# A head that takes the cosine and sine tiles in turn for two rows of x

## The chip, the cores and the metric

The kernel runs on one core of one Trainium2 chip. The core has a matrix engine (TensorE, in the profile PE, with PEld for its weight loads), a vector engine (VectorE, DVE), a scalar engine (ScalarE, ACT), a general engine (GpSimd, POOL) and a sync engine (SP) that only issues transfers. Transfers between the chip's memory and the core's working memory run on 16 DMA engines. The engines run side by side, each takes its own instructions in the order of the program, and they wait for each other through semaphores.

The metric is the device time of one execution in microseconds (us), the median of several.

## The reference

```python
def _A_ref(x, dft_seq_re, dft_seq_im, dft_hid_re, dft_hid_im):
    a = jnp.einsum("bsd,ed->bse", x, dft_hid_re)
    b = jnp.einsum("bsd,ed->bse", x, dft_hid_im)
    return jnp.einsum("ts,bse->bte", dft_seq_re, a) - jnp.einsum("ts,bse->bte", dft_seq_im, b)

def _B_ref(x, w_in, w_sp, b_sp, w_out):
    z = _gelu(jnp.einsum("bsd,df->bsf", x, w_in))
    z1, z2 = z[..., :Fh], _layernorm(z[..., Fh:], axis=-1)
    g = jnp.einsum("ts,bsf->btf", w_sp, z2) + b_sp[None, :, None]
    return jnp.einsum("bsf,fd->bsd", z1 * g, w_out)

mod = (_silu(c) @ w_mod).reshape(c.shape[0], 6, 1, -1)
sa, ca, ga, sb, cb, gb = ...
h = _layernorm(x, axis=-1) * (1 + ca) + sa
x = x + ga * _A_ref(h, ...)
h = _layernorm(x, axis=-1) * (1 + cb) + sb
x = x + gb * _B_ref(h, ...)
```

x has 2048 positions of 512 features. The first half mixes with two Fourier matrices, the second half is a gated two-layer network. Everything is float32.

## The kernel before

The first stage multiplies the normed x from the left with the cosine and the sine matrix over positions (2048 x 2048 each). x is handled in 16 "rows" s of 128 positions (X[s], 128 x 512). The matrices come in blocks of 512 x 512 (list src, in turn cosine and sine for a group of four rows; block b lies in stage[b], two buffers). A block holds four tiles k of 128 positions; tile n is the unit of the stage: `squares` transposes it from the block on DVE into T[n] (tag t, two buffers), ACT copies it to a rounded high part AH[n] (four buffers), DVE subtracts to get the low part AL[n] (three buffers). The row of x is split in the same way into h_hi[s] and h_lo[s]. Tile n then takes twelve matmuls: for each of four feature blocks high times high, high times low, low times high, added in four PSUM banks per matrix (GP). With t = 0, tiles 0 to 3 are the cosine with rows 0 to 3, tiles 4 to 7 the sine with rows 0 to 3, tiles 8 to 11 the cosine with rows 4 to 7, and so on.

Tile 0 alone isn't split (WHOLE = 1): its four matmuls take T[0] and the normed row in plain float32, which the profile shows as eight passes.

The order on each engine is written by hand (a manual schedule). Ahead of the loop stands the head, lines 1087 to 1122. It issues transfers on SP (some on ACT's queue, through `two`): row 0 of x, half of the first cosine block, row 1, rows 2 and 3, the other half, the first sine block (load(1)), rows 4 and 5. `keep_busy` puts matmuls of ones on PE until the data is there. `stats_first` takes mean and variance of a row on DVE, the power −1/2 on POOL, and the shift on DVE (row 0) or POOL. `whole_first(0)` norms row 0 on ACT; `hi_first`, `norm_x`, `lo_h` make the two parts of rows 1 to 3; `split_first(0)` and `rest_first(0)` make those of row 0, at the end of the head.

Then the loop runs over n: `prep(n)` prepares tile n + 3's high and tile n + 2's low part unless the head has done so, `mm_a(n)` issues the matmuls, and `run(n)` the work that `at(n, ...)` has put there: at 0 the load of rows 6 and 7 (load_x(1, range(2, 4))), at 2 the row c, at 4 the stats of rows 4 and 5 and the load of rows 8 to 11, at 6 the stats of rows 6 and 7 and the high parts of rows 4 and 5, at 7 the low parts of rows 4 and 5. The last tile of a block, in prep_hi, frees its buffer and issues load(b + 2). So load(2) is issued in the head (prep_hi(3)) and load(3) in the loop (prep_hi(7), at n = 4).

```python
        if not N2 <= n < N4 and k == 3:
            stage.pop(b)
            if b != NB0:
                load(b + 2)
```

Of the kernel before, what the change touches and what calls it, by code (L numbers as in the profile page):

```python
# [13 lines left out]
P = 128  # L14
# [6 lines left out]
def fnet_gmlp_kernel(  # L21
# [125 lines left out]
    NE = N4 + 4 * NQ * len(PROD)  # L147
    NB = {p: N4 + 4 * NQ * i for i, p in enumerate(PROD)}
    NB0 = len(src) + 2
    stage, T, AH, AL = {}, {}, {}, {}  # L150

    def load_block(tile_, a, s0=0, s1=P):
        v = a.rearrange("(b j) (a s) -> a j b s", j=32, a=4)
        for q in range(4):
            nc.sync.dma_start(tile_[32 * q:32 * q + 32, :, s0:s1], v[q][:, :, s0:s1])

    def load_half(tile_, a, h, engs=(nc.sync,) * 4):

        v = a.rearrange("(b j) (a s) -> a j b s", j=32, a=4)
        for q in range(4):  # L160
            engs[q].dma_start(tile_[32 * q:32 * q + 32], v[q][:, :, 64 * h:64 * h + 64])
# [3 lines left out]
    def load(b):  # L165
        if b < len(src):
            stage[b] = blocks.tile([P, 16, P], F32, tag="stage", bufs=2, name=f"stage{b}")
            load_block(stage[b], src[b])
        elif b < len(src) + 2:
            j = b - len(src)  # L170
            XB.append(blocks.tile([P, 4, Q], F32, tag="stage", bufs=2, name=f"xb{j}"))
            for g in range(2):
                nc.sync.dma_start(XB[j][:, 2 * g:2 * g + 2], ht_d[g].rearrange("(k p) t -> p k t", p=P)[:, 2 * j:2 * j + 2])
                for kk in range(2):
                    TT[2 * j + kk, g] = XB[j][:, 2 * g + kk]
        elif 4 * (b - NB0) < NE - N4:
            i, gh = divmod(b - NB0, NQ)
            g, h = divmod(gh, 2)
            p = PROD[i]
            stage[b] = blocks.tile([P, 2, 16, 64], F32, tag="stage", bufs=2, name=f"stage{b}")  # L180
            for r in range(2):
                load_half(stage[b][:, r], s_d[S_OF[p], r, g] if p in S_OF else
                          quad(w_sp, r + (2 if p == 4 else 0), g + (2 if p == 1 else 0)), h)
# [5 lines left out]
    def squares(dst, block, k):  # L189
        nc.vector.transpose(dst.rearrange("p (b i) -> p b i", i=32), block[:, :, 32 * k:32 * k + 32])  # L190
# [61 lines left out]
    def prep_hi(n):  # L252
        if n >= NE or n in highs:
            return
        highs.add(n)
        if N2 <= n < N4:
            T[n] = form_t(n)
        else:
            b, k = divmod(n, 4) if n < N2 else (NB0 + (n - N4) // 4, (n - N4) % 4)
            if b != NB0:  # L260
                T[n] = blocks.tile([P, Q], F32, tag="t", bufs=2, name=f"t{n}")
            if b == NB0:
                assert n in T
            elif n >= N4:
                squares(T[n], stage[b][:, k % 2], k // 2)
            else:
                squares(T[n], stage[b], k)
        AH[n] = SE[2][:, n - N4] if N4 <= n < N4 + 4 else blocks.tile([P, Q], F32R, tag="ah", bufs=4, name=f"ah{n}")
        nc.scalar.activation(AH[n], T[n], AF.Copy)  # L269
        if not N2 <= n < N4 and k == 3:  # L270
            stage.pop(b)
            if b != NB0:
                load(b + 2)
# [91 lines left out]
    def keep_busy(n, k):  # L365

        ps = bank(k, "busyp")
        for _ in range(n):
            nc.tensor.matmul(ps, ones, busy, start=True, stop=True)

    def fold_sum(t, w, u):

# [49 lines left out]
    def load_x(g, ks=range(4), eng=nc.sync):  # L422

        if g not in XG:
            XG[g] = spool.tile([P, 4, D], F32, tag="x", bufs=2, name=f"x{g}")
        k0, k1 = ks[0], ks[-1] + 1
        v = x.rearrange("(g a k i) d -> g a i k d", g=NQ, a=4, i=32)
        for a in range(4):
            eng.dma_start(XG[g][32 * a:32 * a + 32, k0:k1, :], v[g, a][:, k0:k1, :])
        for k in ks:  # L430
            X[4 * g + k] = XG[g][:, k, :]
# [4 lines left out]
    def stats_first(s):  # L436

        m = spool.tile([P, 12], F32, tag="first", bufs=4, name=f"first{s}")
        nc.vector.bn_stats(m[:, :6], X[s])
        mv = m[:, 8:]  # L440
        nc.vector.bn_aggr(mv[:, :2], m[:, :6])
        nc.vector.tensor_scalar(mv[:, 1:2], mv[:, 1:2], EPS, None, op0=ALU.add)
        nc.gpsimd.tensor_tensor(mv[:, 2:3], mv[:, 1:2], mhalf, op=ALU.pow)
        eng = nc.gpsimd if s else nc.vector
        eng.tensor_scalar(mv[:, 3:4], mv[:, 0:1], mv[:, 2:3], -1.0, op0=ALU.mult, op1=ALU.mult)
        NRM[s] = mv[:, 2:3], mv[:, 3:4]

    two = (nc.sync, nc.sync, nc.scalar, nc.scalar)
# [1 line left out]
    def load_two(k):  # L450
        if not k:
            XG[0] = spool.tile([P, 4, D], F32, tag="x", bufs=2, name="x0")
        v = x.rearrange("(g a k i) d -> g a i k d", g=NQ, a=4, i=32)
        for a in range(4):
            two[a].dma_start(XG[0][32 * a:32 * a + 32, k, :], v[0, a][:, k, :])
        X[k] = XG[0][:, k, :]

    def whole_first(s):

        LN[s] = spool.tile([P, D], F32, tag="xn", bufs=4, name=f"xn{s}")  # L460
        nc.scalar.activation(LN[s].rearrange("p (k a i) -> p k a i", a=4, i=32),
                             X[s].rearrange("p (a k i) -> p k a i", a=4, i=32), AF.Identity,
                             bias=NRM[s][1], scale=NRM[s][0])
        nc.scalar.activation(LN[s][:, :1], ones[:, :1], AF.Copy)

    def split_first(s):
# [3 lines left out]
    def rest_first(s):  # L470
        hh, hl = [h.rearrange("p k m -> p (k m)") for h in (h_hi[s], h_lo[s])]
        nc.gpsimd.tensor_tensor(hl, LN[s], hh.bitcast(F32), op=ALU.subtract)

    def turn_whole(n):
        T[n] = blocks.tile([P, Q], F32, tag="t", bufs=2, name=f"t{n}")
        squares(T[n], stage[0], n)
        highs.add(n)
        lows.add(n)
# [23 lines left out]
    def ones_x(s):  # L502
        LN[s] = spool.tile([P, D], F32, tag="xn", bufs=4, name=f"xn{s}")
        nc.gpsimd.memset(LN[s][:, 0:1], 1.0)
# [27 lines left out]

    def mm_a(n):
        t, r = divmod(n, 8 * NQ)
        j, s = ((r // 4) % 2, r // 8 * 4 + r % 4) if t == 0 else (r // NS, r % NS)
        if s == 0:
            for k in range(ND):
                GP[t, j, k] = bank(4 * j + k if t == 0 else ring[0] % 6, f"gp{t}_{j}_{k}")
                ring[0] += t > 0
        if n < WHOLE:  # L540
            a, b = LN.pop(s), T.pop(n)
            for k in (1, 2, 3, 0):
                nc.tensor.matmul(GP[0, 0, k], a[:, k * P:(k + 1) * P], b, start=s == 0, stop=False)
            return
        ah, al = AH.pop(n), AL.pop(n)
        if n < 4:
            for a, b in ((h_hi[s], ah), (h_hi[s], al), (h_lo[s], ah)):
                for k in (1, 2, 3, 0):
                    nc.tensor.matmul(GP[0, 0, k], a[:, k, :], b, start=False, stop=False)
            return  # L550
        for k in range(ND):
            matmul3(GP[t, j, k], h_hi[s][:, k, :], h_lo[s][:, k, :], ah, al, s == 0, s == NS - 1)
        if s == NS - 1:
            for k in range(ND):
                ps = GP.pop((t, j, k))
                gt_hi[t, j, k] = GP_[0].tile([P, Q], F32R, tag=f"gh{j}_{k}", name=f"gh{t}_{j}_{k}")
                gt_lo[t, j, k] = GP_[0].tile([P, Q], F32R, tag=f"gl{j}_{k}", name=f"gl{t}_{j}_{k}")
                split(gt_hi[t, j, k], gt_lo[t, j, k], ps)
# [526 lines left out]


    load_two(0)
    stage[0] = blocks.tile([P, 16, P], F32, tag="stage", bufs=2, name="stage0")
    load_half(stage[0][:, :, :64], src[0], 0, two)
    load_two(1)  # L1090
    nc.scalar.activation(sc, ones[:, :ND], AF.Silu)
    load_x(0, range(2, 4))
    load_half(stage[0][:, :, 64:], src[0], 1)
    load(1)
    load_x(1, range(2))
    keep_busy(3, 5)
    ones_x(1)
    ones_x(2)
    ones_x(3)
    stats_first(0)  # L1100
    whole_first(0)
    turn_whole(0)
    prep_hi(1)
    stats_first(1)
    prep_lo(1)
    hi_first(1)
    stats_first(2)
    norm_x(1)
    stats_first(3)
    hi_first(2)  # L1110
    lo_h(1)
    prep_hi(2)
    norm_x(2)
    prep_hi(3)
    prep_lo(2)
    lo_h(2)
    hi_first(3)
    norm_x(3)
    prep_lo(3)
    split_first(0)  # L1120
    rest_first(0)
    lo_h(3)
    at(0, load_x, 1, range(2, 4))
    at(2, load_row)
    at(9, silu_row)
# [324 lines left out]
```

## Time and profile before

| | us |
|---|---|
| median of three runs | 931.37 |
| the runs | 932.79, 931.37, 931.15 |
| the profiled execution | 931.77 |
| its span, first to last instruction | 930.0 |
| PE busy | 924.2 |
| DVE busy | 738.2 |
| ACT busy | 409.1 |
| POOL busy | 199.1 |

The span is what the trace covers, the time of an execution what the device reports for it. Start times in the trace count from the span's start. "Busy" of PE is the union of its matmuls, whose ends are modelled. In a row of a timeline stand the start, the duration (of the group, if several instructions are merged), the engine, the line, the operation with the tiles it writes and reads, the count, and in brackets how long the engine stood idle before it and what ended that. SPq and ACTq rows are issues of transfers.

### The profile page before, as it was taken

What the parts mean: (1) busy time and instruction counts of PE and PEld (TensorE: products, weight loads), DVE (VectorE), ACT (ScalarE), POOL (GpSimd) and SP (SyncE); (2) the same over time, 40 slices, a digit from 0 to 9 for tenths busy, and PEclk for the clock granted to TensorE, in tenths of its full rate; (3) what the DMA queues carried; (4) which work ended last, traced back from release to release, by engine and by line L of the source; (5) the groups of instructions that cost most, each with busy time, mean ns of one, the idle gap of its engine ahead of it and who ended that gap; (6) DMA issues with size and microseconds to landing.
All of it is one profiled execution on the core that took longest, in us unless ns stands there. A gap on an engine that the chain in (4) does not pass through costs nothing.

```text
span 930.0 us, 12339 instructions
## 1 busy us (share of the span) xinstructions
PE 924.2 (99%) x4053; PEld 760.4 (82%) x4053; DVE 738.2 (79%) x1218; ACT 409.1 (44%) x733; POOL 199.1 (21%) x375
## 2 busy tenths in 40 slices
PE   9999999999999999999999999999999999999998
PEld 5888888888888888888888888888888888888887
DVE  7799968787687677875678788899799789986762
ACT  5694424232132222322577877674544544331121
POOL 2330000224554165323512321331000000000000
PEclk9999999999999999999999999999999999999999
DMA  9995762856639977996463864444464566734651
GB/s 218 225 227 118 142 158 46 193 147 171 158 91 319 283 220 217 275 343 227 141 217 130 279 201 103 118 105 105 105 146 102 130 142 143 178 97 149 185 178 57
DMA packets 246976, 157.88 MB, mean 170 GB/s; under 512 B 140384, under 2 KB 214368, under 8 KB 246784
## 3 DMA queue, kind: packets, MB, share of 16 engines
q1 hardware_dynamic: 233248, 119.57, 52.2%
q0 software_dynamic: 12272, 36.86, 11.4%
q8 instruction: 32, 0.52, 0.2%
q10 hardware_dynamic: 1392, 0.66, 0.2%
q14 instruction: 32, 0.26, 0.1%
HBM read 120.33 MB, written 36.71 MB: 169 GB/s over the span
## 4 chain that ended last, share of the span: by engine, by line
PE 98%; DMA 1%; SPq 0%; ACTq 0%; DVE 0%; ACT 0%; issue 0%; DVEq 0%
PE gp L99 12%; PE gp L97 12%; PE gp L98 12%; PE gw L99 10%; PE gw L97 10%; PE gw L98 10%; PE yp L99 3%; PE yp L98 3%; PE yp L97 3%; PE op L98 3%; PE op L97 3%; PE op L99 3%; PE fp L98 1%; PE fp L97 1%; PE fp L99 1%; PE z2s L98 1%
## 5 line engine op out<-in xcount | busy, mean ns | idle before, releaser
L269 ACT ACTIVATE ah<-t 128x512 fp32r<-128x512 f32 x235 | 148.5, 632 | 362.6 <-DVE t L190 242.7
L287 DVE TENSOR_TENSOR al<-t,ah 128x512 fp32r<-128x512 f32 x235 | 160.6, 683 | 55.7 <-PE gp L98 30.9
L98 PE MATMUL gp<-al,hh 128*128 128x512 f32 x496 | 193.0, 389 | 0.0
L97 PE MATMUL gp<-ah,hh 128*128 128x512 f32 x496 | 193.0, 389 | 0.0
L99 PE MATMUL gp<-ah,hl 128*128 128x512 f32 x496 | 193.0, 389 | 0.0
L190 DVE STREAM_TRANSPOSE t<-stage 128x512 f32<-128x512 f32 x236 | 165.5, 702 | 6.3 <-DMA stage<-in_A_dft_seq_re_dram 3.1
L98 PE MATMUL gw<-al,bh 128*128 128x512 f32 x400 | 155.6, 389 | 0.0
L99 PE MATMUL gw<-ah,bl 128*128 128x512 f32 x384 | 149.5, 389 | 0.0
L97 PE MATMUL gw<-ah,bh 128*128 128x512 f32 x384 | 149.4, 389 | 0.0
L98 PEld LDWEIGHTS gp<-al,hh 128*128 128x128 f32 x496 | 93.1, 188 | 19.5 <-DVE al L287 0.2
L97 PEld LDWEIGHTS gp<-ah,hh 128*128 128x128 f32 x496 | 93.1, 188 | 19.4
L99 PEld LDWEIGHTS gp<-ah,hl 128*128 128x128 f32 x496 | 93.1, 188 | 19.3
L98 PEld LDWEIGHTS gw<-al,bh 128*128 128x128 f32 x400 | 75.1, 188 | 15.7
L99 PEld LDWEIGHTS gw<-ah,bl 128*128 128x128 f32 x384 | 72.1, 188 | 15.3 <-DVE bl L948 0.3
L97 PEld LDWEIGHTS gw<-ah,bh 128*128 128x128 f32 x384 | 72.1, 188 | 14.9
L920 POOL DMA_DIRECT2D s_d<-sj x64 | 35.1, 548 | 107.2 <-DVE sj L912 82.3
L97 PE MATMUL yp<-hth,gh 128*128 128x512 f32 x128 | 49.8, 389 | 0.0
L98 PE MATMUL yp<-htl,gh 128*128 128x512 f32 x128 | 49.8, 389 | 0.0
L99 PE MATMUL yp<-hth,gl 128*128 128x512 f32 x128 | 49.8, 389 | 0.0
L665 POOL DMA_DIRECT2D ht_d<-hturn x62 | 41.0, 667 | 23.1 <-DVE hturn L661 18.2
L97 PE MATMUL op<-woh,uh 128*128 128x512 f32 x110 | 42.8, 389 | 0.0
L98 PE MATMUL op<-wol,uh 128*128 128x512 f32 x110 | 42.8, 389 | 0.0
(247 smaller groups left out, 1449.4 us busy)
## 6 DMA issues: line engine op xcount, KB each, us to landing
stage<-in_A_dft_seq_im_dram SPq DMA_DIRECT2D x64, 256.0 KB, 6.0
sj<-in_B_w_sp_dram SPq DMA_DIRECT2D x32, 512.0 KB, 7.2
s_d<-sj POOLq DMA_DIRECT2D x64, 256.0 KB, 4.7
stage<-s_d SPq DMA_DIRECT2D x128, 128.0 KB, 2.9
stage<-in_A_dft_seq_re_dram SPq DMA_DIRECT2D x60, 256.0 KB, 5.6
stage<-in_B_w_sp_dram SPq DMA_DIRECT2D x88, 128.0 KB, 3.0
wm<-in_w_mod_dram SPq DMA_DIRECT2D x16, 256.0 KB, 6.1
xr<-in_A_x_dram POOLq DMA_DIRECT2D x16, 256.0 KB, 4.5
```

The lines of the kernel that those rows point to most:

```text
L97: nc.tensor.matmul(acc, ah, bh, start=first, stop=False, skip_group_check=go_on)
L98: nc.tensor.matmul(acc, ah, bl, start=False, stop=False, skip_group_check=go_on)
L99: nc.tensor.matmul(acc, al, bh, start=False, stop=last, skip_group_check=go_on)
L190: nc.vector.transpose(dst.rearrange("p (b i) -> p b i", i=32), block[:, :, 32 * k:32 * k + 32])
L269: nc.scalar.activation(AH[n], T[n], AF.Copy)
L287: nc.vector.tensor_tensor(AL[n], t, AH[n].bitcast(F32), op=ALU.subtract)
L665: eng.dma_start(v[a, i], ht[32 * a:32 * a + 32].rearrange("c (b r) -> c b r", r=32))
L920: nc.gpsimd.dma_start(s_d[m, r, g][b * P:(b + 1) * P, :], a)
```

## The change

The first eight tiles get an order of their own, FRONT, as pairs (matrix j, row s): cosine 0, sine 0, cosine 1, sine 1, cosine 2, cosine 3, sine 2, sine 3. The transfers follow it: row 0 of x, a quarter of the cosine block, half of the sine block, row 1, the second quarter, rows 2 and 3, the two remaining halves, rows 4 and 5. The normed row 0 is written in three pieces, the factor of the shift moves to POOL for row 0 too, one busy matmul becomes a half, the parts of row 0 are made at once, and `turn_front(n)` turns tiles 1 to 7 at places of their own. What follows a block's last turn stays with it: turn_front(5) issues load(2), turn_front(7) issues load(3), both in the head.

```diff
+    FRONT = ((0, 0), (1, 0), (0, 1), (1, 1), (0, 2), (0, 3), (1, 2), (1, 3))
...
-            b, k = divmod(n, 4) if n < N2 else (NB0 + (n - N4) // 4, (n - N4) % 4)
+            b, k = FRONT[n] if n < len(FRONT) else divmod(n, 4) if n < N2 else (NB0 + (n - N4) // 4, (n - N4) % 4)
...
-        if not N2 <= n < N4 and k == 3:
+        if not N2 <= n < N4 and k == 3 and b in stage:
...
         for _ in range(n):
             nc.tensor.matmul(ps, ones, busy, start=True, stop=True)
+        nc.tensor.matmul(ps[:, :D // 2], ones, busy[:, :D // 2], start=True, stop=True)
...
-        eng = nc.gpsimd if s else nc.vector
-        eng.tensor_scalar(mv[:, 3:4], mv[:, 0:1], mv[:, 2:3], -1.0, op0=ALU.mult, op1=ALU.mult)
+        nc.gpsimd.tensor_scalar(mv[:, 3:4], mv[:, 0:1], mv[:, 2:3], -1.0, op0=ALU.mult, op1=ALU.mult)
...
-        nc.scalar.activation(LN[s].rearrange("p (k a i) -> p k a i", a=4, i=32),
-                             X[s].rearrange("p (a k i) -> p k a i", a=4, i=32), AF.Identity,
-                             bias=NRM[s][1], scale=NRM[s][0])
+        for ks in (slice(1, 2), slice(2, 4), slice(0, 1)):
+            nc.scalar.activation(LN[s].rearrange("p (k a i) -> p k a i", a=4, i=32)[:, ks],
+                                 X[s].rearrange("p (a k i) -> p k a i", a=4, i=32)[:, ks], AF.Identity,
+                                 bias=NRM[s][1], scale=NRM[s][0])
...
+    def turn_front(n):
+        b, k = FRONT[n]
+        T[n] = blocks.tile([P, Q], F32, tag="t", bufs=2, name=f"t{n}")
+        squares(T[n], stage[b], k)
+        if k == 3:
+            stage.pop(b)
+            load(b + 2)
...
-        j, s = ((r // 4) % 2, r // 8 * 4 + r % 4) if t == 0 else (r // NS, r % NS)
+        j, s = FRONT[n] if n < len(FRONT) else ((r // 4) % 2, r // 8 * 4 + r % 4) if t == 0 else (r // NS, r % NS)
...
-        if n < 4:
-            for a, b in ((h_hi[s], ah), (h_hi[s], al), (h_lo[s], ah)):
+        if n < len(FRONT):
+            for i, (a, b) in enumerate(((h_hi[s], ah), (h_hi[s], al), (h_lo[s], ah))):
                 for k in (1, 2, 3, 0):
-                    nc.tensor.matmul(GP[0, 0, k], a[:, k, :], b, start=False, stop=False)
+                    nc.tensor.matmul(GP[0, j, k], a[:, k, :], b, start=s == 0 and i == 0, stop=False)
...
     load_two(0)
-    stage[0] = blocks.tile([P, 16, P], F32, tag="stage", bufs=2, name="stage0")
-    load_half(stage[0][:, :, :64], src[0], 0, two)
-    load_two(1)
+    for b in range(2):
+        stage[b] = blocks.tile([P, 16, P], F32, tag="stage", bufs=2, name=f"stage{b}")
+    load_block(stage[0], src[0], 0, 32, two)
+    load_block(stage[1], src[1], 0, 64, two)
     nc.scalar.activation(sc, ones[:, :ND], AF.Silu)
+    load_x(0, range(1, 2))
+    load_block(stage[0], src[0], 32, 64)
     load_x(0, range(2, 4))
-    load_half(stage[0][:, :, 64:], src[0], 1)
-    load(1)
+    load_block(stage[0], src[0], 64, P)
+    load_block(stage[1], src[1], 64, P)
     load_x(1, range(2))
-    keep_busy(3, 5)
-    ones_x(1)
-    ones_x(2)
-    ones_x(3)
+    keep_busy(2, 5)
+    for s in range(1, 4):
+        ones_x(s)
     stats_first(0)
     whole_first(0)
     turn_whole(0)
+    split_first(0)
+    rest_first(0)
+    turn_front(1)
     prep_hi(1)
     stats_first(1)
     prep_lo(1)
     hi_first(1)
+    turn_front(2)
+    turn_front(3)
+    prep_hi(2)
+    norm_x(1)
+    prep_lo(2)
+    prep_hi(3)
+    lo_h(1)
+    prep_lo(3)
     stats_first(2)
-    norm_x(1)
+    turn_front(4)
+    turn_front(5)
+    prep_hi(4)
+    hi_first(2)
+    prep_lo(4)
+    norm_x(2)
     stats_first(3)
-    hi_first(2)
-    lo_h(1)
-    prep_hi(2)
-    norm_x(2)
-    prep_hi(3)
-    prep_lo(2)
     lo_h(2)
+    prep_hi(5)
+    prep_lo(5)
     hi_first(3)
+    turn_front(6)
+    turn_front(7)
     norm_x(3)
-    prep_lo(3)
-    split_first(0)
-    rest_first(0)
+    prep_hi(6)
     lo_h(3)
+    prep_lo(6)
     at(0, load_x, 1, range(2, 4))
```

More of the change, by code (lines that the diff above doesn't have):

```diff
@@ L149, in fnet_gmlp_kernel, with load_block @@
     NB0 = len(src) + 2
+    FRONT = ((0, 0), (1, 0), (0, 1), (1, 1), (0, 2), (0, 3), (1, 2), (1, 3))
     stage, T, AH, AL = {}, {}, {}, {}
-    def load_block(tile_, a, s0=0, s1=P):
+    def load_block(tile_, a, s0=0, s1=P, engs=(nc.sync,) * 4):
         v = a.rearrange("(b j) (a s) -> a j b s", j=32, a=4)
         for q in range(4):
-            nc.sync.dma_start(tile_[32 * q:32 * q + 32, :, s0:s1], v[q][:, :, s0:s1])
+            engs[q].dma_start(tile_[32 * q:32 * q + 32, :, s0:s1], v[q][:, :, s0:s1])
     def load_half(tile_, a, h, engs=(nc.sync,) * 4):
@@ L258, in prep_hi @@
         else:
-            b, k = divmod(n, 4) if n < N2 else (NB0 + (n - N4) // 4, (n - N4) % 4)
-            if b != NB0:
+            b, k = FRONT[n] if n < len(FRONT) else divmod(n, 4) if n < N2 else (NB0 + (n - N4) // 4, (n - N4) % 4)
+            if n not in T:
                 T[n] = blocks.tile([P, Q], F32, tag="t", bufs=2, name=f"t{n}")
[L262 to L267, printed above, removed]
+                if n >= N4:
+                    squares(T[n], stage[b][:, k % 2], k // 2)
+                else:
+                    squares(T[n], stage[b], k)
         AH[n] = SE[2][:, n - N4] if N4 <= n < N4 + 4 else blocks.tile([P, Q], F32R, tag="ah", bufs=4, name=f"ah{n}")
         nc.scalar.activation(AH[n], T[n], AF.Copy)
-        if not N2 <= n < N4 and k == 3:
+        if not N2 <= n < N4 and k == 3 and b in stage:
             stage.pop(b)
@@ L472, in rest_first @@
         nc.gpsimd.tensor_tensor(hl, LN[s], hh.bitcast(F32), op=ALU.subtract)
+    def turn_front(n):
+        b, k = FRONT[n]
+        T[n] = blocks.tile([P, Q], F32, tag="t", bufs=2, name=f"t{n}")
+        squares(T[n], stage[b], k)
+        if k == 3:
+            stage.pop(b)
+            load(b + 2)
     def turn_whole(n):
```

## The prediction

> **What bounds the kernel now.** I read the page first: busy times, then the chain that ended last.
>
> ```profile
> span 930.0 us, 12339 instructions
> PE 924.2 (99%) x4053; PEld 760.4 (82%) x4053; DVE 738.2 (79%) x1218; ACT 409.1 (44%) x733; POOL 199.1 (21%) x375
> PE 98%; DMA 1%; SPq 0%; ACTq 0%; DVE 0%; ACT 0%; issue 0%; DVEq 0%
> ```
>
> TensorE (PE) is the bound, and the change alters none of the matmuls behind the first eight tiles. So I asked where PE ever waits: the view of PE's waits, then busy time by stretch.
>
> ```profile
> PE busyp L369 <- DVE busy L308: 1.5, 1, 1.5
> PE gp L549 <- ACT ah L269: 0.7, 1, 0.7
> ...
> 13.54:14.25 0.71, 0.00 (x1) 0.00 (x0) 0.61 (x3) 0.68 (x2) 0.00 (x0) 1.00 1.27 232
> 14.26:450.00 435.74, 435.74 (x1922) 360.46 (x1923) 340.54 (x561) 160.79 (x289) 140.76 (x257) 1.00 0.77 197
> ```
>
> PE waits once at the start and once at 13.5, and from 14.26 it streams without a gap. The kernel is therefore a head of 14.26 us and a fixed stream behind it: the change can win what the head loses, and it loses whatever new hole it tears into the stream. The head, in order of time:
>
> ```profile
> 1.53 5.46 PE L369 MATMUL busyp<-busy,ones 128*128 128x512 f32 x6 [1.53 <-DVE busy L308]
> 3.84 0.69 DVE L439 BATCH_NORM_STATS2 first<-x 128x6 f32<-128x512 f32 x1 [2.46 <-DMA x<-in_A_x_dram]
> 4.79 0.15 DVE L442 TENSOR_SCALAR first<-first 128x1 f32<-128x1 f32 x1
> 5.10 0.55 POOL L443 TENSOR_TENSOR first<-first,mhalf 128x1 f32<-128x1 f32 x1 [4.03 <-DVE first L442]
> 5.68 0.21 DVE L445 TENSOR_SCALAR first<-first 128x1 f32<-128x1 f32 x1 [0.74 <-POOL first L443]
> 5.93 0.81 ACT L461 ACTIVATE xn<-x,first 128x512 f32<-128x512 f32 x1 [0.41 <-DVE first L445]
> 6.78 0.20 ACT L464 ACTIVATE xn<-ones 128x1 f32<-128x1 f32 x1
> 6.82 3.85 PE L543 MATMUL gp<-t,xn 128*128 128x512 f32 x8
> 8.32 0.94 POOL L443 TENSOR_TENSOR first<-first,mhalf 128x1 f32<-128x1 f32 x1 [2.67 <-DVE first L442]
> 9.36 0.27 POOL L445 TENSOR_SCALAR first<-first 128x1 f32<-128x1 f32 x1
> 12.47 1.07 PE L549 MATMUL gp<-ah,hl 128*128 128x512 f32 x4
> 12.83 1.30 DVE L190 STREAM_TRANSPOSE t<-stage 128x512 f32<-128x512 f32 x2 [0.69 <-DMA stage<-in_A_dft_seq_re_dram]
> 14.26 1.20 PE L549 MATMUL gp<-ah,hh 128*128 128x512 f32 x4 [0.72 <-ACT ah L269]
> ```
>
> The reader is to see two losses: PE starts real work at 6.82, when the normed row is complete, and it stops before tile 2, because the second half of the cosine block lands only at 12.8.
>
> **The change, part by part.** *Start of tile 0.* The factor of the shift moves from DVE (0.21, started 0.03 behind the power) to POOL (0.27, about 0.1 behind: in the row at 9.36 the power had ended at 8.32 + 0.94 = 9.26). ACT may start at 5.65 + 0.10 + 0.27 + 0.03 = 6.05, 0.12 later. The norm of 512 columns took 0.81 and an activation of one column 0.20, so a piece of 128 columns lies between 0.20 and 0.81; I take 0.35 (0.20 plus a quarter of the rest). PE took the old row before the marker at 6.78 was done, so waits go by region and the first piece is enough: PE starts at 6.45 instead of 6.82. Two and a half busy matmuls in place of three end near 5.9 instead of 6.8 and don't delay it. A busy pass takes 5.46/6 = 0.91, a real one 3.85/8 = 0.48: the first run at half the clock, so 0.37 earlier is worth about 0.2. The quarter block is half the bytes of the old half and isn't late for 6.4; its 128-byte runs in this place no row shows (cost per byte between the old one and twice it, where the quarter lands when the half did, before 5.96).
>
> *The hole at 13.5.* Matmuls follow at (1.07 − 0.39)/3 = 0.227, so PE was free at 13.38 and the hole costs 0.88, and the group behind it 0.13 more (1.20 against 1.07). In the new order tile 1 takes the sine half with the same row of x. That half is the third transfer, all loaded by about 7; ah follows at 8.5, hh of row 0 at 7.9, hl from POOL (1.29, in the fence below) at 9.3, al behind the stats of row 1 at 9.8. Tile 0 ends at 10.3, so tile 1 runs 10.3 to 13.0. Tile 2 reuses t's first buffer (two in all), so its transpose waits for tile 0: 10.5. Then, each by its row:
>
> ```profile
> L269 ACT ACTIVATE ah<-t 128x512 fp32r<-128x512 f32 x7 | 4.4, 630 | 3.9 <-DVE t L190 3.9
> L483 ACT ACTIVATE hh<-x,first 128x512 fp32r<-128x512 f32 x3 | 2.4, 811 | 1.8 <-DMA stage<-in_A_dft_seq_re_dram 1.7
> L121 ACT ACTIVATE xn<-x,first 128x511 f32<-128x511 f32 x3 | 2.4, 801 | 0.0
> 17.69 1.29 POOL L472 TENSOR_TENSOR hl<-xn,hh 128x512 fp32r<-128x512 f32 x1 [4.78 <-ACT hh L468]
> L443 POOL TENSOR_TENSOR first<-first,mhalf 128x1 f32<-128x1 f32 x4 | 3.1, 769 | 7.7 <-DVE first L442 7.6
> ```
>
> Turns 2 and 3 to 11.8; ah 2 to 12.2, norm of row 1 to 12.9, ah 3 to 13.5; al 2 to 13.0, hl 1 to 13.7, al 3 to 14.2; stats of row 2 (1.0, as from 3.84 to 4.94), **turns 4 and 5 to 16.5**; ah 4 to 16.5, hh 2 to 17.3, al 4 to 17.3, stats of row 3 to 18.2, hl 2 behind its norm to 18.9, al 5 to 19.5, **turns 6 and 7 to 20.7**. PE wants tile 2 at 13.0 (al at 13.9, hl at 14.8), tile 4 at 18.5, tile 5 at 21.2: the smallest margin is about 0.6, no wait. Gain so far 0.88 + 0.13 + 0.2 = **1.2 us**, and tile 8 would start at 29.4.
>
> *SP's queue, where the price lies.* Eight more issues (x row 1 and the second quarter as 64 KB pieces, the sine block as two halves) cost SP some 8 × 0.43 = 3.4 us, beside transfers that are under way. What isn't hidden is an order: turn_front(5) and turn_front(7) now issue load(2) and load(3) **before** the loop's load_x(1, 2:4), which brings rows 6 and 7 of x. Before, rows 6 and 7 went ahead of load(3):
>
> ```profile
> 14.16 3.32 SPq L155 DMA_DIRECT2D stage<-in_A_dft_seq_re_dram x4
> 17.57 3.19 SPq L429 DMA_DIRECT2D x<-in_A_x_dram x4
> 22.78 2.67 SPq L155 DMA_DIRECT2D stage<-in_A_dft_seq_im_dram x4
> ...
> L429 SPq DMA_DIRECT2D x<-in_A_x_dram x4: 425/427/1775, 17.6 to 20.3; - x4
> DMA to landing us min/median/max: 5.4/5.7/6.7
> ...
> 18.00:22.00 4.00, 4.00 (x19) 3.26 (x19) 3.82 (x7) 1.91 (x4) 0.98 (x1) 1.00 1.24 226
> 22.00:26.00 4.00, 4.00 (x19) 3.31 (x18) 3.90 (x8) 1.71 (x3) 2.17 (x6) 1.00 1.08 227
> 26.00:30.00 4.00, 4.00 (x19) 3.33 (x18) 3.93 (x9) 3.56 (x7) 2.26 (x8) 1.00 1.23 231
> 2.00:6.00 4.00, 4.00 (x6) 1.35 (x5) 1.28 (x5) 1.56 (x3) 0.55 (x1) 1.00 0.96 251
> ```
>
> The last piece of rows 6 and 7 was issued at 20.3 and landed some 5.9 later, at 26.2. The engines were full (226 to 231 GB/s), so load(3)'s 1.05 MB ahead of it cost 1.05/0.228 = 4.6 us: 30.8. Bounds: if the 3.67 MB before load(2) move at 251 GB/s, up to 1.0 sooner: 29.7. If SP's small issues (64 KB in 0.43 is 152 GB/s) starve the engines between 5 and 8, some 0.6 later: 31.4. load(2) can't go before turn 5 (16.5, it was 14.16), nor load(3) before turn 7 (20.7), which takes away most of the early end. I take **30.5**.
>
> Who waits: the stats of rows 6 and 7 stand on DVE ahead of hl of row 4, which tile 8 needs:
>
> ```profile
> 26.62 0.68 DVE L105 BATCH_NORM_STATS2 bstx<-x 128x6 f32<-128x512 f32 x1
> 27.44 0.66 DVE L105 BATCH_NORM_STATS2 bstx<-x 128x6 f32<-128x512 f32 x1
> 28.24 0.68 DVE L190 STREAM_TRANSPOSE t<-stage 128x512 f32<-128x512 f32 x1
> 28.84 0.65 DVE L287 TENSOR_TENSOR al<-t,ah 128x512 fp32r<-128x512 f32 x1
> 29.41 1.28 DVE L525 TENSOR_TENSOR hl<-xn,hh 128x512 fp32r<-128x512 f32 x2
> ...
> 31.22 0.39 PE L99 MATMUL gp<-ah,hl 128*128 128x512 f32 x1
> ```
>
> From the first of these stats to the end of hl of row 4 are 29.41 − 26.62 + 0.69 = 3.48, behind which PE follows by 0.05. The third matmul of tile 8, the first to use that hl, ran at 31.22 before. Now: landing 30.5, stats 30.6, hl ready 34.1, matmul at 34.15. As PE streams before and behind it, the kernel moves by 34.15 − 31.22 = **+2.9 us**. The head's gain doesn't enter: PE only waits 1.3 longer for the same hl. Instructions behind it (al 10, x rows 8 and up, load(4)) have the same bytes ahead of them as before and a later PE, so no second wait.
>
> **The sum.** The profiled execution took 931.77 for its span of 930.0, 0.4 above the median of 931.37. I put the difference on the median: 931.4 + 2.9 = **934.3 us**; by the bounds of the landing (29.7 to 31.4, +2.1 to +3.8) 933.5 to 935.2. Below 0.2% (1.86 us) a measurement of this kernel can't be told from no change.
>
> **The rivals.** *No hole at tile 8 (not slower).* Rows 6 and 7 would have to land by about 26.2, so that hl is ready when PE, now early, wants it at 29.85. Then only the head counts: 931.4 − 1.2 = 930.2. For it: in the old order DVE had 1.1 to spare (hl ready at 30.10, used at 31.22). Against it: they can't even be issued before turn 7 and four issues of load(3), 20.7 + 2.0, and 4.6 us of transfers lie ahead on full engines. 0.07. *A shorter hole:* a landing before 29.4 gives +1.7 or less, some 932.6, which also counts as no change: 0.10.
>
> *The clock falls in the hole.* PE would stand still from about 29.85 to 34.15, 4.3 us. In this trace it never stood still for over 0.9 once the clock was up, so no row shows what happens. If it falls, PE runs at half speed until it rises again; at the start that took from 1.53 to between 6.8 and 7.5, about 5.6 us, so at most 2.8 more: 934.3 to 937.1. The Trainium skill ("TensorE: Matmul & The Clock Gate", Part 1) says that the array drops to half clock after an idle window of about 3.4 us, in windows that run freely; by that rule one hole of 4.3 us in four holds a whole window, (4.3 − 3.4)/3.4 as an estimate, and no run here shows it yet. I give it 0.10. *The clock rises late at the start,* because PE now idles from 5.9 to 6.45 before it is up: tile 0 at 0.85 a pass would end near 13.3, and turns 5 and 7, load(3) and rows 6 and 7 come up to 3 later: about 936.5. 0.04.
>
> *The pieces don't start PE early* (the matmul waits for the whole row, near 7.3): the wait at tile 8 swallows most of it, at most +0.3; it lies in the forecast.
>
> **How the numbers follow.** Forecast 0.65, clock rivals 0.14, other new waits 0.02: slower 0.81. Shorter hole and no hole: same 0.17. Faster by over 1.86 us would need more than the head can lose in the rows: 0.02. The range goes from 932.4, inside the shorter hole, to 936.6, inside the clock rivals.
>
> **What would show it.** First real matmul near 6.45; no PE wait before 20 us; load(2) issued near 16.5, load(3) near 20.7, rows 6 and 7 behind them; the stats of row 6 on DVE waiting for x until about 30.6; one PE wait of about 4 us at L99, released by DVE's hl. Wrong if rows 6 and 7 land before 27, or if PE waits elsewhere in the first 20 us.

## The result and the profile after

| | us |
|---|---|
| changed kernel, median of five runs | 939.53 (939.50 to 940.59) |
| kernel before, median of five runs | 931.28 (931.11 to 932.79) |
| ratio | 1.0088, 95% interval 1.0074 to 1.0103 |
| profiled execution of the changed kernel | 939.66, span 937.9 |

The change costs 8.2 us, 0.9%; 2.9 were forecast, and the range ended at 936.6. The page of the changed kernel:

```profile
span 937.9 us, 12357 instructions
PE 925.8 (99%) x4053; PEld 761.8 (81%) x4053; DVE 738.2 (79%) x1217; ACT 409.5 (44%) x735; POOL 201.4 (21%) x376
PE 95%; DVE 2%; DMA 1%; SPq 1%; ACT 0%; issue 0%; POOL 0%; ACTq 0%; DVEq 0%; POOLq 0%
```

PE is busy 1.6 us longer with the same 4053 matmuls, and PE's share of the chain that ended last falls from 98% to 95%, mostly to DVE (2%) and to issues on SP (1%). The changed kernel's waits on PE (engine, tile and line, what releases it; total us, count, longest), then its PE in order of time, and last the one line of the kernel before that belongs beside it:

```profile
PE gp L99 <- DVE hl L533: 6.2, 1, 6.2
PE busyp L368 <- DVE busy L307: 1.5, 1, 1.5
PE gw L99 <- DVE bl L956: 0.4, 1, 0.4
PE gp L551 <- ACT xn L461: 0.3, 1, 0.3
```

```profile
6.49 3.70 PE L551 MATMUL gp<-t,xn 128*128 128x512 f32 x8 [0.35 <-ACT xn L461]
...
29.53 0.39 PE L97 MATMUL gp<-ah,hh 128*128 128x512 f32 x1
29.75 0.39 PE L98 MATMUL gp<-al,hh 128*128 128x512 f32 x1
36.37 0.79 PE L99 MATMUL gp<-ah,hl 128*128 128x512 f32 x1 [6.22 <-DVE hl L533]
```

```profile
30.77 0.39 PE L97 MATMUL gp<-ah,hh 128*128 128x512 f32 x1
```

Tile 8 starts at 29.53 instead of 30.77: the head wins the 1.24 that was forecast. Then its third matmul waits for hl of row 4 and runs at 36.37 instead of 31.22. SP's issues and DVE show why:

```profile
17.03 1.91 SPq L156 DMA_DIRECT2D stage<-in_A_dft_seq_re_dram  x4
21.36 2.44 SPq L156 DMA_DIRECT2D stage<-in_A_dft_seq_im_dram  x4
23.84 2.41 SPq L429 DMA_DIRECT2D x<-in_A_x_dram  x4
```

```profile
32.83 0.69 DVE L105 BATCH_NORM_STATS2 bstx<-x 128x6 f32<-128x512 f32 x1 [5.04 <-DMA x<-in_A_x_dram]
33.56 0.18 DVE L107 BATCH_NORM_AGGREGATE mvx<-bstx 128x2 f32<-128x6 f32 x1
33.66 0.66 DVE L105 BATCH_NORM_STATS2 bstx<-x 128x6 f32<-128x512 f32 x1
34.36 0.18 DVE L107 BATCH_NORM_AGGREGATE mvx<-bstx 128x2 f32<-128x6 f32 x1
34.45 0.68 DVE L191 STREAM_TRANSPOSE t<-stage 128x512 f32<-128x512 f32 x1
35.06 0.65 DVE L286 TENSOR_TENSOR al<-t,ah 128x512 fp32r<-128x512 f32 x1
35.63 1.28 DVE L533 TENSOR_TENSOR hl<-xn,hh 128x512 fp32r<-128x512 f32 x2
```

load(2), load(3), rows 6 and 7, in this order. DVE stands still for 5.04 us until row 6 is there, and hl of row 4 is queued behind. The last part of the loss is in PE's clock. In the view by stretches, the third figure from the end is the granted clock (1.00 is full speed):

```profile
32.00:34.00 2.00, 0.00 (x0) 0.00 (x0) 1.13 (x3) 0.00 (x0) 0.17 (x1) 0.93 1.06 202
34.00:36.00 2.00, 0.00 (x0) 0.00 (x0) 1.97 (x5) 0.77 (x2) 1.65 (x5) 0.50 1.08 223
...
38.00:40.00 2.00, 2.00 (x7) 1.52 (x6) 0.82 (x2) 1.49 (x3) 0.00 (x0) 0.50 1.24 226
40.00:41.00 1.00, 1.00 (x5) 0.82 (x4) 0.32 (x1) 0.12 (x1) 0.00 (x0) 0.73 1.26 221
41.00:45.00 4.00, 4.00 (x19) 3.30 (x18) 3.69 (x8) 1.77 (x4) 0.00 (x0) 1.00 1.25 229
```

By the shares 0.93 and 0.73 of the two mixed stretches, PE has half its clock between about 33.7 and 40.5. From 36.4 on it works, so 4.2 us of work are worth 2.1. The account, from one profiled execution to the other: 36.37 − 31.22 = 5.15 for the hole less the head's gain, 2.1 for the clock, about 0.65 for the wait at L956 (at 814 us) and the slower groups around it. That makes 7.9 = 937.9 − 930.0.

### The profile page after: what moved, and what is told of

It reads as the page before. It is cut to its first block, busy times and chain, and to the rows that moved or that the text cites. A ratio compares the mean times of both kernels' runs of the same rounds, so it can differ in the third digit from the quotient of the medians.

```text
span 937.9 us, 12357 instructions
## 1 busy us (share of the span) xinstructions
PE 925.8 (99%) x4053; PEld 761.8 (81%) x4053; DVE 738.2 (79%) x1217; ACT 409.5 (44%) x735; POOL 201.4 (21%) x376
## 4 chain that ended last, share of the span: by engine, by line
PE 95%; DVE 2%; DMA 1%; SPq 1%; ACT 0%; issue 0%; POOL 0%; ACTq 0%; DVEq 0%; POOLq 0%
PE gp L99 12%; PE gp L97 12%; PE gp L98 12%; PE gw L99 9%; PE gw L97 9%; PE gw L98 9%; PE yp L99 3%; PE yp L98 3%; PE yp L97 3%; PE op L99 3%; PE op L97 3%; PE op L98 3%; PE fp L98 1%; PE fp L97 1%; PE fp L99 1%; PE z2s L98 1%
## 5 line engine op out<-in xcount | busy, mean ns | idle before, releaser
L99 PE MATMUL gp<-ah,hl 128*128 128x512 f32 x480 | 187.7, 391 | 6.2 <-DVE hl L533 6.2
L98 PE MATMUL gp<-al,hh 128*128 128x512 f32 x480 | 187.5, 391 | 0.0
L97 PE MATMUL gp<-ah,hh 128*128 128x512 f32 x480 | 187.5, 391 | 0.0
L99 PE MATMUL gw<-ah,bl 128*128 128x512 f32 x384 | 149.6, 390 | 0.4 <-DVE bl L956 0.4
L99 PEld LDWEIGHTS gp<-ah,hl 128*128 128x128 f32 x480 | 90.6, 189 | 25.4 <-DVE hl L533 6.6
L98 PEld LDWEIGHTS gp<-al,hh 128*128 128x128 f32 x480 | 90.5, 189 | 19.0 <-DVE al L286 0.2
L97 PEld LDWEIGHTS gp<-ah,hh 128*128 128x128 f32 x480 | 90.6, 189 | 18.9
L99 PEld LDWEIGHTS gw<-ah,bl 128*128 128x128 f32 x384 | 72.1, 188 | 16.0 <-DVE bl L956 1.1
L99 PE MATMUL yp<-hth,gl 128*128 128x512 f32 x128 | 49.8, 389 | 0.0
```

The lines of the kernel that those rows point to most:

```text
L97: nc.tensor.matmul(acc, ah, bh, start=first, stop=False, skip_group_check=go_on)
L98: nc.tensor.matmul(acc, ah, bl, start=False, stop=False, skip_group_check=go_on)
L99: nc.tensor.matmul(acc, al, bh, start=False, stop=last, skip_group_check=go_on)
```

## The experiments

Theory A: SP's order (rows 6 and 7 behind load(3)), handed on by DVE's order, makes the hole, and the fall of the clock is a second term that the hole brings with it. Rival B: the new order of tiles or the slower transfers of the new head make the loss by themselves. Each kernel ran beside the kernel before on the same chip.

| kernel | median, us | before, us | ratio, 95% interval |
|---|---|---|---|
| e1 rows 6 and 7 first | 932.34 | 931.25 | 1.0011 (1.0002 to 1.0020) |
| e2 stats of rows 6 and 7 later | 936.84 | 931.25 | 1.0055 (1.0042 to 1.0069) |
| e3 hole filled | 937.53 | 931.25 | 1.0064 (1.0050 to 1.0077) |
| e4 old head, order swapped | 938.41 | 931.25 | 1.0079 (1.0063 to 1.0094) |
| e5 e1, longer busy work | 932.13 | 931.28 | 1.0009 (1.0000 to 1.0018) |
| e6 e5, one half block | 932.09 | 931.28 | 1.0008 (0.9999 to 1.0017) |
| e7 e6, stats later too | 932.61 | 931.28 | 1.0013 (1.0004 to 1.0022) |
| e8 half block alone | 939.15 | 931.28 | 1.0080 (1.0066 to 1.0094) |
| e9 e6, stats of rows 2 and 4 early | 930.89 | 931.47 | 0.9994 (0.9985 to 1.0003) |
| e10 e5, stats of row 4 early | 931.90 | 931.47 | 1.0006 (0.9997 to 1.0015) |

### The order, taken out of the new head and put into the old one (e1, e4)

```diff
 # e1, in the changed kernel
     turn_front(5)
+    load_x(1, range(2, 4))
...
-    at(0, load_x, 1, range(2, 4))
```

> The changed kernel with rows 6 and 7 of x issued right behind load(2), ahead of load(3). If the order on SP's queue is the cause, they land some 2.2 us behind load(2) (25.1 in the changed kernel's trace), near 27.3 instead of 32.7; the stats run at 27.4, the low part of row 4 is ready near 30.9, PE waits about 1 us at tile 8 instead of 6.4 and the clock stays up: 31.0 against 31.2 before for the third matmul of tile 8, so about 931.0 us. If the loss lies in the other parts of the change (the new order of tiles, slower transfers), the time stays above 936.

```diff
 # e4, in the kernel before
-    at(0, load_x, 1, range(2, 4))
-    at(2, load_row)
+    at(4, load_x, 1, range(2, 4))
+    at(4, load_row)
```

> The kernel before with one thing moved: rows 6 and 7 of x (and the row c) are issued behind load(3) instead of ahead of it, by the same loop step that issues the stats of row 4. If the order alone makes the hole, rows 6 and 7 land 1.05 MB / 0.228 later, 26.2 + 4.6 = 30.8, and the third matmul of tile 8 starts at 30.8 + 3.65 = 34.45 instead of 31.22: 931.3 + 3.2 = 934.5 us, up to 2 more if the clock falls in a hole of 3.2 us. If the new head is needed for it, it stays at 931.3.

One moved load takes 7 of the 8 us away from the new head (rows 6 and 7 land by 26.9 in e1), and the same load moved the other way, with the small row c behind it, brings 7 us into the old one. PE's waits in e4, and its DVE in order of time:

```profile
PE gp L99 <- DVE hl L525: 5.0, 1, 5.0
```

```profile
32.04 0.69 DVE L105 BATCH_NORM_STATS2 bstx<-x 128x6 f32<-128x512 f32 x1 [6.12 <-DMA x<-in_A_x_dram]
```

So A holds, and B falls as the account of the 8 us: the new head isn't needed for the hole. But two sizes are off. In e4 the rows land near 31.9 instead of 30.8, the hole is 5.0 instead of 3.2, and the clock falls, so the time is 938.4 instead of 934.5. And e1 is 932.3 instead of 931.0: the head's gain doesn't come back. That is taken up below.

### Where the late landing turns into a wait (e2)

```diff
 # e2, in the changed kernel
-        at(n, stats_x, s)
+        at(n + (s in (6, 7)), stats_x, s)
```

> The changed kernel with the stats of rows 6 and 7 one step later, behind the low parts of rows 4 and 5; SP's order is left as it is. If DVE's order is what hands the late landing on to tile 8, PE doesn't wait at tile 8; it waits at tile 10 instead, whose row 6 lands at 32.7 and is ready some 4.6 us later, about 37.3 against 35.0 wanted: 2.3 us lost, 1.2 won in the head, the clock stays up: about 932.4 us. If tile 8 waits for something else that is late (its own tile, the block), the wait stays there and the time is above 936.

The wait goes from tile 8 to tile 10, as expected: DVE's order is what hands it on. PE's waits in e2, PE in order of time around the wait, and the stretches behind it:

```profile
PE gp L97 <- ACT hh L528: 2.7, 1, 2.7
```

```profile
34.80 0.39 PE L99 MATMUL gp<-ah,hl 128*128 128x512 f32 x1
37.92 0.50 PE L97 MATMUL gp<-ah,hh 128*128 128x512 f32 x1 [2.74 <-ACT hh L528]
```

```profile
38.00:39.00 1.00, 0.93 (x3) 0.49 (x4) 1.00 (x3) 1.00 (x4) 0.00 (x0) 1.00 1.25 247
39.10:42.40 3.30, 3.30 (x9) 2.62 (x8) 3.23 (x8) 1.05 (x2) 0.83 (x3) 0.50 1.24 236
42.50:45.00 2.50, 2.50 (x13) 2.05 (x12) 1.59 (x3) 1.95 (x4) 1.53 (x6) 1.00 1.22 238
```

The time missed by 4.4. The expectation let the clock stay up in a hole of 2.3 us; from one matmul to the next passed 3.12 us (a wait of 2.7), and from 1 us after the hole the clock was at half for some 3.4 us (1.7 lost). The clock and the longer hole make about 2.1 of the 4.4. The profiled execution of e2 took 935.89, less than the others of its runs (up to 936.98); the rest of the difference isn't settled.

### The clock by itself (e3)

```diff
 # e3, in the changed kernel: between the second and third matmul of tile 8
+                for _ in range(27):
+                    nc.tensor.matmul(GP[t, j, k], zeros, ah, start=False, stop=False)
```

> The changed kernel with 27 matmuls by a zero tile (27 x 0.227 = 6.1 us) between the second and the third matmul of tile 8, so that PE is busy in the hole; they add zeros. If the fall of the clock is a term of its own, the clock stays at 1.00, the third matmul starts near 36.4 as before and the 4.2 us of work at half speed behind it become 2.1: 937.4 us. If the half clock costs nothing (PE would have waited for DVE anyway), it stays at 939.5.

The tile zeros is filled by ACT in step 1 of the loop. The time is 937.53, against 937.4 expected. The third matmul starts at 36.02, as late as in the changed kernel (36.37, less 0.35), and the stretch behind it runs at full speed. PE of e3 in order of time, and the view by stretches:

```profile
29.90 6.28 PE L564 MATMUL gp<-ah,zeros 128*128 128x512 f32 x27
36.02 0.39 PE L565 MATMUL gp<-ah,hl 128*128 128x512 f32 x1
```

```profile
36.00:40.00 4.00, 4.00 (x19) 3.32 (x18) 3.69 (x7) 3.51 (x7) 0.33 (x3) 1.00 1.22 233
```

The fall of the clock is a term of its own: the medians are 939.53 − 937.53 = 2.0 apart.

### What keeps the head's gain back (e5, e6, e7)

In e1's profiled execution the first real matmuls ran at half clock until 10.6, and PE wasn't early at tile 8 at all:

```profile
6.67 5.62 PE L551 MATMUL gp<-t,xn 128*128 128x512 f32 x8 [0.53 <-DVE t L191]
...
31.67 0.39 PE L99 MATMUL gp<-ah,hl 128*128 128x512 f32 x1
```

Eight passes took 5.62 instead of 3.70. The theory now was that the idle time ahead of them (0.74 us from the end of the busy work at 5.93) kept the clock down, and that this is why e1 gains nothing. e5 tests it; e6 tests whether the small rows of the quarters matter.

```diff
 # e5 = e1 and
-        nc.tensor.matmul(ps[:, :D // 2], ones, busy[:, :D // 2], start=True, stop=True)
+        nc.tensor.matmul(ps[:, :384], ones, busy[:, :384], start=True, stop=True)
 # e6 = e5 and
-    load_block(stage[0], src[0], 0, 32, two)
+    load_block(stage[0], src[0], 0, 64, two)
-    load_block(stage[0], src[0], 32, 64)
 # e7 = e6 and the line of e2
```

> Rows 6 and 7 ahead of load(3), and the last busy matmul takes 384 columns instead of 256, so that at half clock the busy work ends near 6.35 instead of 5.93 and PE idles some 0.3 us before the first real matmul, not 0.74. If that idle time kept the clock down until 10.6 in the run with rows 6 and 7 first (3.43 us later than before, worth 1.7 us), the clock is up by 8.4 at the latest and the time falls to 930.3 to 931.0 us. If the idle time has nothing to do with it, the clock rises late in some executions as before and the median stays near 932.3.

> The last kernel with the first half of the cosine block loaded in one piece with rows of 256 bytes, as before the change, instead of two quarters with rows of 128. If the quarters' small rows and the four extra issues put the stream of transfers behind (1.65 against 1.92 MB moved by 10 us), rows 2 to 7 land about 1 us sooner (rows 6 and 7 near 25.9) and tile 0 starts at most 0.2 later: 930.2 us. If the quarters cost nothing, rows 6 and 7 land at 26.9 again and the time is that of the last kernel within 0.2.

> The last kernel with the stats of rows 6 and 7 behind the low parts of rows 4 and 5 as well. If DVE's order still held tile 8 up by a few tenths, they go: 930.1 us, 1.2 below before. If there is nothing left to wait for at tile 8, the time is that of the last kernel.

None brought the gain that it was to bring: 932.1, 932.1, 932.6. In e5 the first real matmul ran at full clock at once, and yet PE waited 1.3 us at tile 8, so a late clock isn't what holds e1. What the idle time does to the clock, e5 doesn't show: in its profiled execution the passes became short during the busy work (from 4.7 us on), which therefore ended early, and PE idled 1.1 us ahead of tile 0, longer than in e1. The answer stands in e6, where rows 6 and 7 land by 26.5. PE's waits in e6, and its DVE from the low part of row 3 on:

```profile
PE gp L99 <- DVE hl L533: 1.0, 1, 1.0
```

```profile
22.69 0.69 DVE L533 TENSOR_TENSOR hl<-xn,hh 128x512 fp32r<-128x512 f32 x1 [0.85 <-ACT xn L121]
23.30 0.69 DVE L286 TENSOR_TENSOR al<-t,ah 128x512 fp32r<-128x512 f32 x1
...
28.13 0.69 DVE L105 BATCH_NORM_STATS2 bstx<-x 128x6 f32<-128x512 f32 x1
...
30.91 1.28 DVE L533 TENSOR_TENSOR hl<-xn,hh 128x512 fp32r<-128x512 f32 x2
```

The reader is to see the bracket that is missing: at 28.13 DVE doesn't wait for x, as it did at 32.83 above. It has worked without a break since 22.69 and reaches the stats of row 6 at 28.13, 1.5 later than in the old head (26.62). hl of row 4 is ready at 30.91 + 0.69 = 31.60, PE wanted it at 30.5. The third matmul of tile 8 runs at 31.65 instead of 31.22, which is 0.4 of the 1.0 us by which e6's span is longer than before (931.0); the rest goes at one more short wait, for DVE's al at 102.8 (0.3, and slower groups around it). DVE's own chain is a second bound, right behind the transfers. In e7 PE waits at tile 10 instead (1.1 us, released by ACT's hh of row 6), since the same work is only done in another order.

### DVE's chain, shortened (e9, e10)

```diff
 # e9 = e6 and (e10 = e5 and only the second of these)
     turn_front(3)
+    stats_first(2)
...
     turn_front(7)
+    stats_x(4)
     norm_x(3)
 # and both taken out at their old places
```

> The kernel with rows 6 and 7 first, the longer busy work and one half block, and two pieces of DVE's work put where DVE waits: the stats of row 2 behind turn_front(3) (1.1 us idle before al of tile 2) and the stats of row 4 behind turn_front(7) (0.85 us idle before hl of row 3). With the rows landed at 26.5, DVE works without a break from 22.7 to hl of row 4 at 31.6; PE wants that at 30.5. If DVE's own chain is what now holds tile 8, it comes some 1.5 us sooner, the wait of 1.0 us at tile 8 goes, and the time falls by 1 to 1.3: 930.8 to 931.1 us. If something else holds PE, the wait stays and the time stays near 932.1.

> The kernel with rows 6 and 7 first and the longer busy work, quarters as in the change, and only the stats of row 4 moved into DVE's wait behind turn_front(7). DVE would reach the stats of row 6 0.8 us sooner, at 27.2, but the rows land between 26.9 and 27.6, so 0.4 to 0.8 comes off the wait of 1.3 at tile 8: 931.4 to 931.7 us. If DVE's chain has no part in it, 932.1.

e9 is at 930.89, inside its expectation; the wait at tile 8 is gone, and hl of row 4 comes 1.7 us sooner than in e6. DVE of e9 in order of time, and what is left among PE's waits:

```profile
29.22 1.28 DVE L533 TENSOR_TENSOR hl<-xn,hh 128x512 fp32r<-128x512 f32 x2
```

```profile
PE gp L98 <- DVE al L286: 0.2, 1, 0.2
PE gp L557 <- ACT ah L268: 0.2, 1, 0.2
```

e10 takes 0.5 off the wait (0.8 instead of 1.3), inside the 0.4 to 0.8 expected; its median missed by 0.2. So DVE's chain was the second bound. e9 is the only version with a median below both kernels, 0.6 below before, and its interval still holds 1. Its PE is 0.9 ahead of before shortly before 100 us and only 0.4 ahead after it: behind the matmul at 100.6 it waits for DVE's al, which runs at 100.44, as in the old kernel (100.36). What ties DVE to that time wasn't followed up.

### The small rows (e8)

> The changed kernel with only the two quarters put back to one half, rows 6 and 7 still behind load(3). If the small rows are what made the landing of rows 6 and 7 later than the 30.5 that was forecast (32.7 was measured, and 31.9 with the old head), they land near 31.2, the hole at tile 8 is about 5 us instead of 6.4 and the clock still falls: about 938 us. If the small rows have no part in it, they land between 31.9 and 32.7 again: 938.7 to 939.5 us.

e8 is the changed kernel with only e6's two lines. Rows 6 and 7 land later still, near 33.2, and the time is 939.15, inside the second branch. The small rows alone don't account for the late landing. Stretches of e8, and its issues on SP:

```profile
14.00:18.00 4.00, 4.00 (x20) 3.28 (x19) 3.76 (x8) 1.34 (x4) 0.81 (x2) 1.00 0.74 178
18.00:20.00 2.00, 2.00 (x10) 1.68 (x9) 1.86 (x5) 1.97 (x5) 0.16 (x1) 1.00 0.37 107
```

```profile
17.97 1.91 SPq L156 DMA_DIRECT2D stage<-in_A_dft_seq_re_dram  x4
```

Without the quarters the transfers ahead of load(2) are through sooner, and then the engines stand nearly empty from 17 to 19 us (4 and 3 GB/s; 107 on the mean from 18 to 20), because load(2) isn't issued before turns 4 and 5 have run (16.64 to 17.94). With the quarters about as much time is lost in a slower stream. Two waits lie beside each other; taking one away shows the other.

## Why the prediction was wrong

- **The head's gain: right in size, in part by luck.** Tile 8 starts 1.24 earlier (1.2 forecast), with the first real matmul at 6.49 (6.45), and as forecast the gain ends at the wait for hl. But two errors cancel in it. At tile 2 PE was 1.47 ahead (12.79 against 14.26), where 0.88 + 0.2 had been added up; and 0.23 was lost again after that, mostly at 21.2, where the weight load waited 0.5 us for hh of row 3; the prediction saw no wait there, with a smallest margin of 0.6. (Its 29.4 for the start of tile 8 is a slip too: 30.77 − 1.2 is 29.57.)
- **The mechanism: right.** load(2) at 17.03 (16.5), load(3) at 21.36 (20.7), rows 6 and 7 behind them, DVE waiting for them, one wait at L99 released by hl. From the first stats to the matmul 36.37 − 32.83 = 3.54 (3.53).
- **The landing of rows 6 and 7: mis-sized, the first failed term.** Taken 30.5 with bounds 29.7 to 31.4; DVE's stats, which it released, began at 32.83, so it was about 32.7. 4.6 us were charged for load(3)'s 1.05 MB on engines that are always full at 228 GB/s. In the old head alone the order costs 31.9 − 26.2 = 5.7 (e4): load(3), now ahead, has to wait for turn 7 and goes at 21.14, so SP issues nothing from 16.7 on, and the stream from 22 to 32 us ran at 195 to 244. In the changed kernel the last piece of rows 6 and 7 was issued at 25.8 instead of 20.3 and landed 6.9 us later instead of 5.9: 5.5 of the 6.5 us lie ahead of the issue, and only 1.0 behind it. The new head adds 0.8 to e4's 5.7: its stream was slower from the start, in the rows of the changed kernel and, in the last line, of the kernel before (last column, GB/s):

```profile
2.00:6.00 4.00, 4.00 (x6) 1.35 (x5) 1.42 (x4) 1.55 (x3) 0.82 (x2) 1.00 1.04 214
6.00:10.00 4.00, 3.65 (x10) 1.63 (x9) 2.54 (x6) 2.78 (x6) 1.67 (x2) 1.00 0.88 179
```

```profile
6.00:10.00 4.00, 4.00 (x9) 1.60 (x8) 3.46 (x7) 1.92 (x4) 1.20 (x2) 1.00 0.74 207
```

  The prediction allowed 0.6 us for small issues; (251 + 207 − 214 − 179) x 4 us = 0.26 MB behind at 10 us are 1.1 us already. That the slower stream makes the 0.8 isn't shown: e8, which was ahead at 10 us, landed later still. This term makes 2.2 of the 5.2 us that were missed.
- **The clock: the second failed step.** It stood as a rival with 0.10, beside the forecast and on the forecast's hole of 4.3. It fell in the profiled execution of every kernel with a hole of 2.7 or more (changed, e2, e4, e8) and in none with 1.3 or less. All the executions on record say the same by their mean clock: 0.995 to 0.998 in every one of these four kernels, 0.999 or 1.000 in every one of the others. In the changed kernel it costs 2.0 to 2.1. So it belonged into the sum and not beside it: the forecast's own hole of 4.3 is longer than e2's, which brought the clock down in all four executions, and the 0.10 was too low even against the prediction's own estimate of one hole in four. The range took the two errors one at a time and ended below both together.
- **The rival "no hole", 930.2: wrong in its premise.** With the rows in time (e6: 26.5) the time is 932.1, since DVE reaches hl of row 4 only at 31.6. The prediction followed DVE's queue up to turn 7 and then took the old kernel's distance from landing to hl, without asking when DVE itself would be there.
- **"The clock rises late at the start", 0.04:** it happened in e1's profiled execution (10.6). There it cost little that DVE's chain hadn't taken already: hl of row 4 was ready at 31.39 and the matmul that takes it ran at 31.67.
- **"No second wait":** nearly. PE stood 0.35 at L956, at 814 us, which the prediction had no term for; similar short waits come and go there in e1 and e3, and they weren't followed up.

## What to carry over

When an issue moves earlier on an in-order queue, list what now stands behind it, down to the last small load that an engine will wait for, and price the landing with the gate of the issue (here a buffer's last reader), not with bytes alone. When a wait on PE is forecast, price the clock with it: in these runs every hole of 2.7 us or more also put PE at half clock for 3.4 us or longer. And a gain at the start of the bound engine counts only up to the next engine's chain: look for the second bound before adding it to a sum.

## What the runs showed of the hardware that was not expected

- The clock falls in shorter holes than assumed. In e2 PE went 3.12 us from one matmul's start to the next (wait 2.7) and the clock fell. The Trainium skill ("TensorE: Matmul & The Clock Gate", Part 1) tells of an idle window of about 3.4 us. The hole here was too short to hold one, so by this measurement a window that is idle for the greater part is enough. Waits of 0.7 (before) and 1.3 (e5) left it up.
- A fall lasted about 3.4 us in the profiled executions of e2 and e4 and about 6.8 in those of the changed kernel and e8. In e2 PE was back at work before the clock fell and stayed at work. By the mean granted clock of the single executions (0.998 or 0.996) both lengths occur with one and the same kernel, as an estimate: 3.4 us at half clock take 0.002 off the mean of 936 us, 6.8 take 0.004.
- In e1, PE's idle time of 0.74 us ahead of tile 0 went with a clock that rose at 10.6 instead of about 7; the column of the granted clock has no record before the rise and shows 1.00 there, so the time of a pass (0.85 or 0.43) is what tells it. The idle time isn't shown to be the cause: in e8's profiled execution PE idled longer at this place (a wait of 0.98 against 0.53 in the same view), and the first real matmul ran at full clock.
